# A state-space scan and a low-rank mixer on one Trainium2 core: the same steps in another listed order

## The chip, the cores and the metric

The kernel runs on one core of one Trainium2 chip. The metric is the device time of one execution in microseconds (us); the median of several executions counts, and lower is better.

The core has five engines, each with its own queue that it works off in order: PE (TensorE, matrix products; the profile shows the load of the stationary operand apart as PEld), DVE (VectorE), ACT (ScalarE), POOL (GpSimd) and SP (SyncE, which here only issues transfers, or DMAs, between the chip's large memory and the core's). Products land in PSUM, the accumulator memory, which the kernel uses as eight banks.

## What is computed

The reference chains two blocks over 4 batches of 768 tokens.

```python
# scan, per batch and head (8 heads, head_dim 32, d_state 16), in chunks of 32 tokens
cum = np.cumsum(np.log(np.clip(a, 1e-06, 1.0)), axis=-1)      # within the chunk
M = (Cc @ Bc.T) * np.exp(cum_i - cum_j) * (i >= j)
y = M @ xc + (Cc @ state) * np.exp(cum)
state = np.exp(cum[-1]) * state + sum_j(Bc_j * xc_j * np.exp(cum[-1] - cum_j))
# mixer, over x = the scan's output as (batch, 768, 256)
h = x.transpose(0, 2, 1) @ U @ V          # U: 768x32, V: 32x768
u = x + h.transpose(0, 2, 1)
out = u + np.maximum(u @ w_ch1, 0.0) @ w_ch2    # w_ch1: 256x1024, w_ch2: 1024x256
```

All inputs and the output are 32-bit floats.

## The kernel before

**Tiling.** The scan goes through 12 pairs, numbered k = 0 to 11: pair k belongs to batch k // 3 and covers 256 tokens (two blocks of 128). The mixer goes through half batches: batch b, half j (384 tokens). In it the hidden layer of 1024 has eight blocks m of 128.

**The order is written out by hand.** `tc.manual_schedule()` leaves the instructions of every engine in the order in which the program emits them, and the string `PLAN` gives that order as words. `follow(PLAN)` at the end splits it and calls one step a word: the letter picks the step, the numbers its arguments. A step emits instructions for several engines; what it emits is queued on each of them behind what the earlier words emitted there. A step that stands early in the list with its data late thus holds up all that stands behind it on the same engine. The words are:

- `Xk`, `Bk`, `wn` (and with a `Y` ahead `YXk`, `YBk`, `YU0`, `YV0`): loads, issued by SP (line 209). `X` is two transfers, `B` three (two of B, one of C), `w` one piece of a weight, `V` four. A load without `Y` also waits for the last VectorE instruction listed ahead of it (`hold`), which keeps it from running early. The framework gives SP's transfers eight semaphores in turn, so a ninth waits until the first of them has landed.
- `A0`, `A1`, `K0`: the decays from `a` (lines 384 to 411).
- `Pk`, or in parts `Qk.c`: B and C times decay (VectorE). `Tk` (twice), or `Vk.c.v`: PE transposes of that (line 496), copied out by ScalarE or VectorE.
- `sk`: PE products of B and x, the chunk's own state (line 570). `uk`: VectorE carries the state on, three or four instructions, and POOL masks it into `Sm` (line 597).
- `gk`: PE products of C and B (line 536). `mk`, `Mk`: VectorE masks them, two instructions each.
- `nk`, `jk`: PE products of M and x, first and second part (line 686). `ik`: PE products of C and the carried state (line 650). `yk`: ScalarE copies y out of PSUM. `tk`, `O0.0`, `O2.1`: PE turns it to tokens by columns (line 713), copied out by ScalarE, in `O2.1` by VectorE.
- The second part `jk` may run on PE only when the first part is known to have landed. If an instruction of another engine that depends on something after the first part has been emitted in between, that one is waited for. If not, `apart()` emits a copy of one column on POOL (`settled`, line 609) that waits for all products of `nk`, and `jk` waits for that copy.
- `cn` (three times): turns a weight's two 16-bit halves into a 32-bit float again: VectorE and ScalarE first, VectorE second, POOL third (line 439). `c0`, `C0` are the two halves of U and V, `c1` to `c5` pieces of `w_ch1` (`c1`, `c2` half a piece each), `c6` to `c9` pieces of `w_ch2`. `v0` spreads V (line 893). `Rn` (two or three times) splits a weight into three parts of type float32r for the up and down products of the later halves: ScalarE, POOL (line 453), VectorE.
- `pb`, `qb`: PE products with U and a second one that brings them to all rows (lines 739, 747, 757). `ab.j`: product with V; VectorE adds x to it, which gives u in `yT`.
- `U0.0.m`: the up product of block m for the first half of batch 0, in plain 32 bits (line 801). `Sb.j`: u in three parts. `fb.j.m`: up product of three parts, six PE instructions; `hb.j.m`: VectorE finishes what its relu leaves. `db.j.k.n`: the n-th piece of the down product for 128 tokens; the last piece is followed by a VectorE sum and the transfer of the output.
- `En`: n products of the 128 x 128 identity with n blocks of itself in one instruction (line 139), into a PSUM bank that is not read. They compute nothing that is used.

What one engine needs of another it waits for by semaphores that the framework places.

**Buffers.** Each PSUM tile takes its bank from the string `BANKS`, in the order of emission, and each staging tile of 4 KB a row (`words()`) takes one of 15 slots from `SLOTS`. A new tile waits until the last reader of the old one in its place is done. `u` in three parts has one buffer, which the plain copy of `w_ch1` holds until the products `U0.0.m` and the splits `R0` to `R3` are done.

The list before the change begins (the middle is left out):

```python
PLAN = (
    'E2 YX0 A1 YB0 A0 Q0.0 Q0.2 YB1 Q0.1 K0 YX1 Q1.0 YB2 V0.0.0 YB3 YX2 V0.1.1 s0 E1 u0 g0 E1 B4 '
...
    'd3.1.1.4 d3.1.2.2 d3.1.0.3 d3.1.2.3 d3.0.2.5 d3.1.1.5 d3.1.2.4 d3.1.2.5 d3.1.0.4 d3.1.0.5 ')
```

## Time and profile before

| | |
|---|---|
| median of 3 executions | 221.96 us (221.53 to 222.24) |
| the profiled execution, whole | 223.1 us |
| its span, first to last instruction | 221.4 us |
| mean clock granted to PE | 0.976 |
| PE busy | 210.0 us, 95% of the span |
| DVE, ACT, POOL busy | 151.7, 87.2, 35.8 us |
| transfers | 14.58 MB in 69663 packets, 63808 of them under 512 bytes |

How to read it: the times of all rows below come from the profiled execution, whose 223.1 us are 1.7 us more than its span and 1.1 us more than the median without the profiler. PE's busy time is a model, since products are pipelined: the start of one product to the start of the next is the better price of a step. The view by stages gives, for each stretch of time, the busy time and the number of instructions of each engine, the clock granted to PE (1.00 is full speed), the mean share of time in which the 16 DMA engines were busy, and GB/s. The view in order of time gives start, duration, engine, line, operation, output<-input, count, and in brackets how long the engine had been idle and whom it waited for.

### The profile page before, as it was taken

What the parts mean: (1) busy time and instruction counts of PE and PEld (TensorE: products, weight loads), DVE (VectorE), ACT (ScalarE), POOL (GpSimd) and SP (SyncE); (2) the same over time, 40 slices, a digit from 0 to 9 for tenths busy, and PEclk for the clock granted to TensorE, in tenths of its full rate; (3) what the DMA queues carried; (4) which work ended last, traced back from release to release, by engine and by line L of the source; (5) the groups of instructions that cost most, each with busy time, mean ns of one, the idle gap of its engine ahead of it and who ended that gap; (6) DMA issues with size and microseconds to landing.
All of it is one profiled execution on the core that took longest, in us unless ns stands there. A gap on an engine that the chain in (4) does not pass through costs nothing.

```text
span 221.4 us, 7025 instructions
## 1 busy us (share of the span) xinstructions
PE 210.0 (95%) x3054; PEld 186.6 (84%) x3054; DVE 151.7 (69%) x314; ACT 87.2 (39%) x196; POOL 35.8 (16%) x47
## 2 busy tenths in 40 slices
PE   7868989989999999999999999998999999999994
PEld 4645755666799799998999999997999999999993
DVE  4775787978987998669734788369315957745722
ACT  2343735768744754414733422133352223214000
POOL 3110036581443800100100010001000000000000
PEclk9995699999999999999999999999999999999999
DMA  6977853889854342216001110000000000010012
GB/s 98 130 100 126 177 175 98 118 135 202 160 153 60 47 95 40 35 52 115 12 0 31 43 50 27 3 24 28 0 3 25 27 24 0 3 47 24 0 50 95
DMA packets 69663, 14.58 MB, mean 66 GB/s; under 512 B 63808, under 2 KB 67840, under 8 KB 69632
## 3 DMA queue, kind: packets, MB, share of 16 engines
q1 hardware_dynamic: 69488, 14.06, 32.2%
q8 instruction: 24, 0.39, 0.7%
q10 hardware_dynamic: 144, 0.07, 0.1%
q14 instruction: 7, 0.06, 0.1%
HBM read 10.98 MB, written 3.15 MB: 64 GB/s over the span
## 4 chain that ended last, share of the span: by engine, by line
PE 74%; DVE 10%; DMA 4%; SPq 4%; issue 2%; POOL 2%; ACT 2%; POOLq 0%; DVEq 0%
PE x L801 34%; PE z L801 24%; DVE words L181 4%; SPq L209 4%; PE y L686 3%; PE y L650 3%; DMA bc<-in_C_dram 2%; PE w L496 2%; PE x L536 2%; DMA bc<-in_B_dram 2%; DVE S L181 1%; PE w L570 1%; DVE M L181 1%; PE w L713 1%; DVE yT L181 1%
## 5 line engine op out<-in xcount | busy, mean ns | idle before, releaser
L181 DVE SCALAR_TENSOR_TENSOR words<-words 128x768 fp32r<-128x768 f32 (+3 forms) x39 | 35.1, 903 | 4.0 <-PE z L801 1.3
L801 PE MATMUL z<-u,w 128*128 128x384 f32 x168 | 34.7, 343 | 0.0
L801 PE MATMUL x<-u,w 128*128 128x384 f32 x168 | 34.3, 342 | 0.0
L801 PE MATMUL x<-w,words 128*128 128x256 f32 x224 | 34.0, 285 | 0.0
L801 PEld LDWEIGHTS x<-w,words 128*128 128x128 f32 x224 | 30.5, 190 | 0.3
L801 PEld LDWEIGHTS z<-u,w 128*128 128x128 f32 x168 | 28.9, 188 | 0.5
L801 PEld LDWEIGHTS x<-u,w 128*128 128x128 f32 x168 | 28.7, 188 | 0.3
L825 ACT ACTIVATE words<-z 128x384 fp32r<-128x384 f32 x28 | 13.8, 492 | 36.0 <-PE z L801 36.0
L825 ACT ACTIVATE words<-x 128x384 fp32r<-128x384 f32 x28 | 13.7, 495 | 32.8 <-PE x L801 32.6
L181 DVE SCALAR_TENSOR_TENSOR words<-x,words 128x384 fp32r<-128x384 f32 x28 | 15.1, 552 | 16.2 <-ACT words L825 14.8
L801 PE MATMUL x<-w2c,words 128*128 128x256 f32 x144 | 25.5, 305 | 0.0
L801 PEld LDWEIGHTS x<-w2c,words 128*128 128x128 f32 x144 | 21.2, 189 | 0.7 <-issue 0.2
L597 POOL TENSOR_TENSOR Sm<-S,own 128x256 f32<-128x256 f32 (+1 forms) x12 | 7.8, 648 | 73.3 <-DVE S L181 73.1
L801 PE MATMUL z<-w,words 128*128 128x256 f32 x112 | 17.9, 287 | 0.5 <-DVE ytok L181 0.5
L181 DVE SCALAR_TENSOR_TENSOR words<-z,words 128x384 fp32r<-128x384 f32 x28 | 15.4, 550 | 3.6 <-ACT words L825 3.6
L801 PEld LDWEIGHTS z<-w,words 128*128 128x128 f32 x112 | 15.6, 189 | 1.2 <-DVE ytok L181 0.8
L181 DVE SCALAR_TENSOR_TENSOR ytok<-x,ytok 128x256 f32<-128x256 f32 (+1 forms) x17 | 6.7, 406 | 10.8 <-PE x L801 10.7
L181 DVE SCALAR_TENSOR_TENSOR S<-S,kept,w 128x64 f32<-128x64 f32 x40 | 11.2, 280 | 3.1 <-PE w L570 1.3
L181 DVE TENSOR_TENSOR BC<-bc,F 128x512 f32<-128x512 f32 (+2 forms) x18 | 10.0, 570 | 4.5 <-ACT F L391 2.1
L686 PE MATMUL y<-M,x 64*32 64x64 f32 x768 | 12.2, 232 | 0.7 <-POOL settled L609 0.6
L686 PEld LDWEIGHTS y<-M,x 64*32 64x32 f32 x768 | 8.9, 110 | 4.6 <-issue 1.8
L801 PE MATMUL z<-w2c,words 128*128 128x256 f32 x72 | 12.7, 306 | 0.0
(137 smaller groups left out, 332.7 us busy)
## 6 DMA issues: line engine op xcount, KB each, us to landing
words<-in_moe_w_ch_dram SPq DMA_DIRECT2D x7, 512.0 KB, 4.4
x<-in_x_dram SPq DMA_DIRECT2D x24, 128.0 KB, 3.2
out_dram<-ytok SPq DMA_DIRECT2D x23, 128.0 KB, 1.7
bc<-in_B_dram SPq DMA_DIRECT2D x24, 64.0 KB, 3.6
bc<-in_C_dram SPq DMA_DIRECT2D x12, 128.0 KB, 3.5
words<-in_moe_w_ch_dram SPq DMA_DIRECT2D x2, 256.0 KB, 4.2
words<-in_moe_U_dram SPq DMA_DIRECT2D x1, 192.0 KB, 3.2
words<-in_moe_V_dram SPq DMA_DIRECT2D x4, 48.0 KB, 2.7
```

The lines of the kernel that those rows point to most:

```text
L181: self.last = call(*args, **kwargs)
L209: op = issuer[0].dma_start(**kwargs)
L496: nc.tensor.transpose(out=tp[:, i, v], in_=s["BC"][:, i, c + v].rearrange("p h n -> p (h n)"), identity=ident)
L536: nc.tensor.matmul(out=s["g"][r][cols, c], lhsT=s["T"][rows, 0, c, cols], rhs=s["Cm"][rows, :, :, ts(2 * c + p, Q)].rearrange("r v t i -> ...
L570: nc.tensor.matmul(out=s["A"][p][ts(r, Q), v], lhsT=s["BC"][half, 0, v, 2 * r:2 * r + 2].rearrange("p h n -> p (h n)"), rhs=x_sb[k][half, ...
L597: nc.gpsimd.tensor_tensor(out=s["Sm"][:, sl], in0=s["S"][:, sl].rearrange("p i (s d) -> p i s d", s=2), in1=own2[:, b, 4 * q + sl.start:4 ...
L650: nc.tensor.matmul(out=channels(k)[r // 2][ts(r % 2, H), c, p], lhsT=own[ts(r, Q)], rhs=st[k]["T"][ts(r, Q), 1, :, ts(2 * c + p, Q)].rearr ...
L686: product = nc.tensor.matmul(out=y[n][ts(i, Q), c, p], lhsT=x_sb[k][half, c, h], rhs=s["M"][half, h // 2, c, h % 2], start=fresh(k, n, [i] ...
L713: nc.tensor.transpose(out=t[:, c, g], in_=yT[b][:, g, ts(2 * q + c, P)], identity=ident)
L801: nc.tensor.matmul(out=t, lhsT=lhsT, rhs=rhs, start=start, stop=True, skip_group_check=True)
L825: nc.scalar.activation(gs[j, m // 2][0][:, m % 2], t, AF.Relu, scale=NEAR)
```

## The change

`PLAN`, `BANKS` and `SLOTS` are replaced; nothing else is. The new list has all the words of the old one, each as often as before, in another order, and in addition three `E1` and one `E2`: products of the identity stand at eight places in place of four. Since PLAN rules all queues, all of PE, DVE, ACT, POOL and SP get a new order. Among what moves:

- The loads begin `X0 B0 B1 B2 B3 U X1 B5 w X2 V` in place of `X0 B0 B1 X1 B2 B3 X2 B4 U w V X3`.
- `g4`, `i3` and `a0.1`, listed ahead of the first `U0.0.m` before, stand behind it; `T5` and `g5` stand ahead of it.
- The eight `U0.0.m`, listed before ahead of `S0.1` and of any down product, now end only after six pieces of the plain down product of batch 0; `S0.1` and the `f0.1.m` follow after all but one of the twelve of these, where before they stood ahead of them.
- The helper `apart()` now emits `settled` eight times in place of three.

```diff
 PLAN = (
-    'E2 YX0 A1 YB0 A0 Q0.0 Q0.2 YB1 Q0.1 K0 YX1 Q1.0 YB2 V0.0.0 YB3 YX2 V0.1.1 s0 E1 u0 g0 E1 B4 '
-    'Q1.2 V1.0.2 m0 YU0 Q1.1 Q2.0 V1.1.2 s1 M0 n0 w0 Q2.2 YV0 u1 g1 m1 M1 i0 X3 Q2.1 w3 V2.0.2 j0 '
-    'y0 V2.1.3 n1 P3 g2 m2 P4 w1 s2 O0.0 M2 T3 T4 c0 u2 T3 i1 T4 j1 i2 c1 y1 g3 c1 n2 E1 j2 C0 y2 '
-    'C0 s3 m3 C0 t1 c0 c0 u3 w2 O2.1 v0 p0 M3 c4 c4 g4 c2 c2 q0 c2 n3 w4 c4 i3 m4 B5 a0.0 X4 c3 R2 '
-    'c3 a0.1 U0.0.1 c1 R2 R0 c3 R1 M4 X5 B6 U0.0.4 U0.0.0 U0.0.5 P5 c5 w6 U0.0.3 T5 T5 s4 j3 c5 R0 '
-    'y3 B8 c5 U0.0.2 u4 g5 R3 w5 i4 M5 X6 U0.0.6 B7 m5 n4 P6 n5 s5 R1 R3 w8 u5 c7 U0.0.7 j4 j5 S0.1 '
...
+    'E1 E1 YX0 A0 YB0 Q0.0 YB1 A1 Q0.2 Q0.1 K0 s0 YB2 YB3 Q1.0 V0.0.0 V0.1.1 Q1.2 YU0 YX1 Q1.1 u0 '
+    'Q2.0 E1 Q2.2 g0 m0 V1.0.2 B5 M0 V1.1.2 w0 V2.0.2 E2 n0 j0 g1 YX2 YV0 m1 i0 E1 P3 E1 M1 Q2.1 c0 '
+    's1 n1 u1 c0 T3 T3 E2 V2.1.3 c1 P5 j1 y0 i1 g2 m2 w1 O0.0 s2 c1 B4 y1 T5 u2 M2 T5 g3 C0 m3 i2 '
+    'n2 E1 X3 c0 j2 M3 y2 C0 c2 t1 C0 w3 c2 O2.1 v0 p0 s3 P4 T4 u3 X4 q0 c2 w2 T4 g5 a0.0 M5 X5 c4 '
+    'w5 m5 n3 c1 U0.0.1 U0.0.0 j3 g4 i3 c4 w6 c4 y3 m4 c3 s4 U0.0.4 R0 t3 U0.0.5 c3 c3 R1 u4 a0.1 '
+    'B6 U0.0.3 M4 c6 i4 w4 n5 c6 R0 n4 w7 c6 s5 U0.0.2 j4 j5 u5 y4 i5 c7 c7 y5 t4 d0.0.1.0 R4 t5 '
+    'd0.0.2.0 R1 p1 c5 d0.0.0.0 c5 w8 B7 c7 d0.0.2.1 P6 c8 T6 c8 R2 c5 X6 c8 R3 c9 T6 c9 q1 c9 '
+    'd0.0.1.1 d0.0.0.1 U0.0.6 U0.0.7 X8 R6 B10 P7 d0.0.1.2 d0.0.2.2 a1.0 R7 T7 T7 R3 d0.0.0.2 '
+    'd0.0.2.3 R2 d0.0.1.3 X9 g6 s6 S0.1 d0.0.0.3 f0.1.2 X10 M6 f0.1.4 f0.1.0 f0.1.1 u6 f0.1.5 R4 B9 '
...
```

## The prediction

> **What bounds the kernel now.** I read the page's busy times first, then stages cut where the work and the clock change, and last the chain and the single rows of the first 40 us.

> ```profile
> span 221.4 us, 7025 instructions
> PE 210.0 (95%) x3054; PEld 186.6 (84%) x3054; DVE 151.7 (69%) x314; ACT 87.2 (39%) x196; POOL 35.8 (16%) x47
> ```

> The stages (times from the start of the span; after each engine its busy time and number of instructions, then the clock, the DMA share and GB/s):

> ```profile
> 5.95:16.20 10.25, 7.67 (x231) 5.43 (x237) 7.59 (x27) 3.65 (x15) 1.50 (x3) 1.00 0.92 115
> 16.20:26.40 10.20, 8.89 (x222) 6.26 (x208) 7.21 (x23) 4.96 (x14) 0.62 (x2) 0.50 0.80 144
> 26.40:37.44 11.04, 9.88 (x293) 6.28 (x289) 8.04 (x24) 6.51 (x19) 4.62 (x7) 1.00 0.39 126
> 37.44:57.00 19.56, 19.00 (x368) 13.02 (x368) 17.70 (x34) 13.95 (x33) 10.05 (x10) 1.00 0.89 161
> 57.00:77.20 20.20, 19.72 (x168) 17.24 (x167) 17.96 (x32) 11.41 (x24) 11.71 (x9) 1.00 0.54 103
> 77.20:94.00 16.80, 16.77 (x173) 16.19 (x174) 13.47 (x25) 7.85 (x16) 1.39 (x2) 1.00 0.31 56
> 94.00:152.00 58.00, 58.00 (x1070) 54.93 (x1073) 39.57 (x83) 19.72 (x44) 2.89 (x5) 1.00 0.16 36
> 152.00:217.20 65.20, 64.61 (x572) 63.81 (x554) 37.01 (x62) 17.20 (x36) 0.97 (x1) 1.00 0.06 20
> ```

> From 37.44 us, where the first `U0.0.m` starts, PE idles 0.56 + 0.48 + 0.03 + 0 + 0.59 = 1.66 us in 179.8 us. There PE is the bound, and a new order of the same products can win little. Ahead of that PE has little to do and waits for data: two stages with 0.92 and 0.80 of the DMA engines busy, and one of 10.2 us at half the clock. So the change is priced by when the first `U0.0.m` starts, and by what is left for PE from there.

> ```profile
> 17.28 4.16 DMA bc<-in_B_dram
> 21.56 0.70 DVE BC L181
> ...
> 37.45 1.44 PE z L801 x4
> ```

> The chain shows a late transfer (`B4`), VectorE behind it, and PE's long run from 37.45 us.

> **The change, part by part.**

> *Loads.* Pair 1's x goes back six places in SP's queue, behind `B2`, `B3` and U; pair 2's x goes behind U, `X1`, `B5` and one w.

> ```profile
> 6.91 1.43 SPq L209 DMA_DIRECT2D x<-in_x_dram  x2
> ...
> 14.37 1.37 SPq L209 DMA_DIRECT2D x<-in_x_dram  x2
> ...
> 20.25 0.49 SPq L209 DMA_DIRECT2D words<-in_moe_w_ch_dram  x1
> 20.79 1.85 SPq L209 DMA_DIRECT2D words<-in_moe_V_dram  x4
> ...
> x<-in_x_dram SPq DMA_DIRECT2D x24, 128.0 KB, 3.2
> ...
> words<-in_moe_V_dram SPq DMA_DIRECT2D x4, 48.0 KB, 2.7
> ```

> Before, `X1` was issued from 6.91 and `X2` from 14.37. By its place in the queue (the DMA engines, not SP, set the pace, at shares of 0.92 and 0.80) `X1` now takes about the places of 13.74 to 14.96, and `X2` those just ahead of the four pieces of V, 20.2 to 20.8. With 3.2 us to landing `X1` is there at about 18 and `X2` at 20.8 + 3.2 = 24.0. `B5` also waits for the last of `m0`, and w and `X2` queue behind it; by its place it is issued about 15.5, later than `m0` can be done, so I cost that at nothing. If `m0` came after 15.5, every load behind it would slip by the difference.

> *From `X2` to the first `U0.0.m`.* What follows `X2` stands in this order on VectorE: `u2 M2 C0 m3 M3 C0`, then POOL's part of `C0`, which ends the conversion of V, then ScalarE's copy, then `v0` on PE.

> ```profile
> 19.83 0.65 PE L570 MATMUL w<-x,BC 64*32 64x64 f32 x24
> ...
> 22.17 0.75 DVE L181 TENSOR_TENSOR M<-z,causal 128x256 int32<-128x256 int32 x2
> ...
> 23.17 0.91 DVE L181 SCALAR_TENSOR_TENSOR S<-S,kept,w 128x64 f32<-128x64 f32 x3
> ...
> 25.19 0.42 DVE L181 TENSOR_SCALAR words<-words 128x192 f32<-128x192 f32 x2
> 25.64 0.36 DVE L181 SCALAR_TENSOR_TENSOR words<-words 128x192 int32<-128x192 int32 x1
> ...
> 28.22 1.26 POOL L439 TENSOR_TENSOR UV<-words 128x192 int32<-128x192 int32 x2
> ...
> 30.16 0.35 ACT L887 CAST Vn<-UV 128x192 fp32r<-128x192 f32 x1
> ...
> 30.56 0.35 PE L893 MATMUL y<-Vn,ident 32*32 32x192 f32 x2 [0.49 <-ACT Vn L887]
> ```

> 24.0 + 0.65 (`s2`) + 0.91 (`u2`) + 3 x 0.75 (`M2`, `m3`, `M3`) + 0.42 + 0.36 (`C0`) + 0.63 (half of the 1.26) + 0.35 (ScalarE) = 29.6, against the 30.56 of before: 1.0 us earlier. From there to the first `U0.0.m` it was 37.44 - 30.56 = 6.88 us. Of that `q0` loses 0.2 us less: `g4` no longer stands ahead of it, and its operand was ready at 33.94.

> ```profile
> 33.55 0.39 ACT L752 ACTIVATE pT<-w 128x256 f32<-128x256 f32 x1
> ...
> 34.16 0.70 PE L757 MATMUL w<-pT,spot 128*128 128x256 f32 x2
> 34.79 0.45 PE L686 MATMUL y<-M,x 64*32 64x64 f32 x32
> 35.17 0.64 PE L650 MATMUL y<-T,Sm 32*64 32x64 f32 x24
> 35.78 0.44 PE L767 MATMUL x<-Vs,ps 128*128 128x384 f32 x1
> ...
> 43.89 0.60 PE L496 MATMUL w<-ident,BC 128*128 128x128 f32 x4
> 44.42 0.45 PE L570 MATMUL w<-x,BC 64*32 64x64 f32 x32
> ```

> So the first `U0.0.m` starts at 36.2: 1.2 us earlier. The bounds: if `X2` is as early as before, V sets the pace, whose last piece is issued by 20.79 + 1.85 = 22.64 and landed by 25.3. With 0.42 + 0.75 + 0.75 + 0.36 + 0.63 + 0.35 behind it `v0` starts at 28.6, 2.0 us earlier, and with the 0.2 of `q0` 2.2 us are won in place of 1.2. The other end is `X2` two places later in the queue, 0.6 us each (1.37 for the two of `X2`): nothing won.

> *What is left for PE from there.* Moved behind it: `g4`, `i3` (35.78 - 35.17 = 0.6) and `a0.1` (0.35, by the two products of `a0.0`, 0.7 at most); moved ahead: `T5` (44.42 - 43.89 = 0.5) and `g5`. The two g cancel. That is 0.6 + 0.35 - 0.5 = 0.45 us more. It lies in PE's bound stage, so all of it counts.

> *Four more instructions of identity products.*

> ```profile
> 3.67 1.06 PE L139 MATMUL w<-ident 128*128 128x256 f32 x2
> ...
> 27.75 0.49 PE L139 MATMUL w<-ident 128*128 128x128 f32 x2
> ```

> Three `E1` at 0.45 to 0.49 and an `E2` at about 1.0: 2.5 us at most. All stand ahead of `X2`'s products or of `j2`, where PE waits: two lie just ahead of `s1`, which now waits for `X1` until 18, and the `E2` ahead of `j1`. I take 0; 2.5 us is the other end, if those waits were gone.

> *Five more `settled` copies on POOL.*

> ```profile
> POOL settled L609 <- PE y L686: 20.6, 3, 12.2
> ...
> PE y L686 <- POOL settled L609: 0.6, 1, 0.6
> ```

> Three cost PE 0.6 us in one place before. Now there are eight, each behind what POOL has listed ahead of it, and on PE all behind `jk` waits. Ends: 0 and 5 x 0.6 = 3.0 us. Those of `j0` to `j2` fall where PE waits for x, `j3` has two `U0.0.m` between its parts, so I take 0, with `j4` as a rival.

> *Half the clock.* Before, full speed in 5.95 to 16.20 with PE 7.67 of 10.25 us busy was followed by 10.2 us at half, and those with 8.89 of 10.20 by full speed to the end. In the new list the identity products fill waits in both stretches, and `s1` and `s2` leave new ones. I take the same state up to 26.4 as before: on the path above only `s2` is PE's, and its 0.65 is a row at half clock.

> ```profile
> PE x L496 <- DVE S L181: 1.1, 1, 1.1
> ```

> [...]

> Sum: -1.2 + 0.45 + 0 + 0 = about -0.75, with the range of the parts mostly on the slow side. The execution of 223.1 us becomes 222.35, and the median without the profiler, 1.1 us below it, 221.96 - 0.75 = 221.2.

> **The rivals.**

> 1. *Slower: half the clock lasts on past 26.4, over `i2` to `a0.0`.* For it: PE now waits for `X1` to 18 and again for `X2` from about 22 to 24, inside the stretch that before was 8.89 of 10.20 busy and earned full speed. Against: the added identity products. On the path are `v0` (32.44 - 30.56 = 1.9), `p0` (1.0), `q0` (0.35 for its two), `a0.0` and half of `j2`, `t1`, `O2.1`: some 3 us that would double: 221.2 + 3 = 224.2. It decides from about 0.75 us of added time, a quarter of that stretch.
> 2. *A new wait: `j4` behind POOL.* Its `settled` is listed behind POOL's part of `c6`, which needs two VectorE steps of `c6`, themselves behind `u4`, `a0.1` and `M4`.

> ```profile
> L439 POOL TENSOR_TENSOR w2c<-words 128x512 int32<-128x512 int32 x4 | 5.8, 1474 | 9.1 <-DVE words L181 7.6 <-ACT words L825 1.5
> ```

> One such step is 1.47 us, and before POOL waited 7.6 us for VectorE at this line. If PE gets to `j4` as POOL begins it, 1.47 us are lost: 222.7. Against: VectorE is less loaded there.

> 3. *Faster: fewer waits from 37 to 77 us.* There VectorE was busy 17.70 + 17.96 of 39.76 us, 90%, and PE idled 0.56 + 0.48. `S0.1` and the `h` steps now come some ten down pieces later, which takes load off VectorE there. If that idle time of 1.04 us goes and V's end of the bounds above holds (1.0 us more), it is 221.2 - 1.0 - 1.0 = 219.2. Against: PE already was 97% busy there.

> **How the numbers follow.** Chances: the forecast, 220.4 to 222.0, 0.42; rival 1 0.23; rival 2 0.13; rival 3 0.22. About 0.3%, 0.66 us, is what a measurement here can tell from no change. The forecast gives faster 0.22 and same 0.2; rival 1 slower; rival 2 slower 0.09, same 0.04; rival 3 faster. Together faster 0.44, same 0.24, slower 0.32. The range runs from rival 3's 219.2, less 0.4 for the spread of the runs shown (221.53 to 221.96), to rival 1's 224.2.

> **What would show it.** Right: `s1` starts at about 18 and `s2` at about 24, waiting for a DMA; `v0` at 29.6 and the first line-801 product at 36.2; PE over 98% busy after it; full clock from 26.4. Wrong: a later half-clock stretch (rival 1); a wait of line 686 for `settled` near 48 us (rival 2); a first `U0.0.m` at 35 or less, or the last product less than 180 us behind it (rival 3).

## The result, and the profile after

The changed kernel takes 219.77 us (median of 7 executions, 218.88 to 220.50), the kernel before 222.20 us in the same call: a ratio of 0.989, with a 95% interval of 0.9854 to 0.9926. (Here and below, a ratio leaves out executions more than 1.5% above the fastest of their kernel, while a median counts them.) The forecast was 221.2 us. The profiled execution took 220.5 us with a span of 218.8, against 223.1 and 221.4 before: 2.6 us less, where the sum of the prediction had 0.75. Line numbers are one higher than before (line 802 is the old 801).

The page's first rows, and the same stages as in the prediction (busy time and count of PE, PEld, DVE, ACT and POOL, then clock, DMA share, GB/s):

```profile
span 218.8 us, 7028 instructions
PE 210.3 (96%) x3062; PEld 187.0 (85%) x3062; DVE 151.0 (69%) x314; ACT 87.7 (40%) x196; POOL 35.6 (16%) x52
```

```profile
5.95:16.20 10.25, 9.15 (x180) 6.47 (x188) 6.15 (x20) 4.95 (x17) 1.38 (x3) 1.00 0.96 128
16.20:26.40 10.20, 9.50 (x291) 6.79 (x276) 7.90 (x26) 4.91 (x14) 1.21 (x3) 1.00 0.61 118
26.40:37.44 11.04, 10.17 (x262) 6.22 (x257) 8.79 (x26) 5.51 (x17) 3.70 (x8) 1.00 0.70 133
37.44:57.00 19.56, 19.02 (x404) 13.38 (x403) 16.08 (x35) 12.70 (x27) 11.07 (x10) 1.00 0.65 175
57.00:77.20 20.20, 20.20 (x193) 17.37 (x191) 17.08 (x29) 12.29 (x26) 10.21 (x9) 1.00 0.81 131
77.20:94.00 16.80, 16.80 (x196) 16.45 (x191) 15.26 (x27) 8.00 (x18) 2.15 (x2) 1.00 0.19 28
94.00:152.00 58.00, 57.55 (x1089) 54.84 (x1088) 39.47 (x82) 21.16 (x49) 3.82 (x7) 1.00 0.14 32
152.00:215.00 63.00, 63.00 (x476) 62.50 (x476) 37.41 (x62) 16.50 (x33) 0.00 (x0) 1.00 0.06 20
```

The stage of 16.20 to 26.40, at half the clock before, is at full speed. PE's idle time between 37.44 and the last product is 0.54 + 0 + 0 + 0.45 + 0 = 0.99 us, against 1.66.

Single rows in order of time, of the changed kernel (PE):

```profile
18.06 0.46 PE L571 MATMUL w<-x,BC 64*32 64x64 f32 x32
...
23.95 0.43 PE L571 MATMUL w<-x,BC 64*32 64x64 f32 x24
...
30.38 0.35 PE L894 MATMUL y<-Vn,ident 32*32 32x192 f32 x2 [0.51 <-ACT Vn L888]
...
36.02 1.21 PE L802 MATMUL z<-yT,w1f 128*128 128x384 f32 x3
...
215.21 0.28 PE L802 MATMUL x<-ps,Vs 128*128 128x256 f32 x1
```

and the last product of the kernel before:

```profile
217.81 0.28 PE L801 MATMUL x<-ps,Vs 128*128 128x256 f32 x1
```

The first `U0.0.m` comes at 36.02 in place of 37.44 (1.42 us earlier). From there to the last product it is 215.21 - 36.02 = 179.19 in place of 217.81 - 37.44 = 180.37 (1.18 less). These are the 2.6 us. The new waits for `settled` are there too (who waited for whom: total, times, longest):

```profile
PE y L687 <- POOL settled L610: 1.3, 3, 0.5
```

So there are three questions: why the clock stayed up, what took 1.18 us out of a stretch that was forecast to grow by 0.45, and what the waits for `settled` cost.

### The profile page after: what moved, and what is told of

Its sections match the earlier page's. It is cut to its first block, busy times and chain, and to the rows that moved or that the text cites. A ratio compares the mean times of both kernels' runs of the same rounds, so it can differ in the third digit from the quotient of the medians.

```text
span 218.8 us, 7028 instructions
## 1 busy us (share of the span) xinstructions
PE 210.3 (96%) x3062; PEld 187.0 (85%) x3062; DVE 151.0 (69%) x314; ACT 87.7 (40%) x196; POOL 35.6 (16%) x52
## 4 chain that ended last, share of the span: by engine, by line
PE 88%; DVE 8%; issue 1%; POOL 1%; DVEq 0%; POOLq 0%
PE x L802 38%; PE z L802 27%; PE y L687 4%; PE y L651 2%; PE x L537 2%; PE w L497 2%; DVE words L182 2%; PE w L714 2%; DVE S L182 2%; DVE M L182 2%; PE w L571 1%; PE w L140 1%; PE x L140 1%; PE w L740 1%; PE z L537 1%
## 5 line engine op out<-in xcount | busy, mean ns | idle before, releaser
L182 DVE SCALAR_TENSOR_TENSOR words<-words 128x768 fp32r<-128x768 f32 (+3 forms) x39 | 35.9, 919 | 5.1 <-PE z L802 3.4
L802 PE MATMUL x<-u,w 128*128 128x384 f32 x168 | 33.8, 340 | 0.0
L802 PE MATMUL z<-u,w 128*128 128x384 f32 x168 | 33.0, 340 | 0.0
L826 ACT ACTIVATE words<-z 128x384 fp32r<-128x384 f32 x28 | 13.7, 491 | 25.3 <-PE z L802 25.3
L802 PE MATMUL z<-w,words 128*128 128x256 f32 x112 | 18.4, 287 | 0.0
L802 PE MATMUL z<-w2c,words 128*128 128x256 f32 x72 | 13.2, 307 | 0.0
L687 PEld LDWEIGHTS y<-M,x 64*32 64x32 f32 x768 | 8.3, 105 | 5.5 <-POOL settled L610 2.8
L687 PE MATMUL y<-M,x 64*32 64x64 f32 x768 | 11.6, 223 | 1.4 <-POOL settled L610 1.3
L182 DVE TENSOR_TENSOR M<-x,causal 128x256 int32<-128x256 int32 x24 | 9.0, 416 | 4.7 <-PE z L537 3.3
## 6 DMA issues: line engine op xcount, KB each, us to landing
x<-in_x_dram SPq DMA_DIRECT2D x24, 128.0 KB, 3.1
out_dram<-ytok SPq DMA_DIRECT2D x23, 128.0 KB, 1.7
bc<-in_C_dram SPq DMA_DIRECT2D x12, 128.0 KB, 3.0
```

The source lines that it names most:

```text
L182: self.last = call(*args, **kwargs)
L687: product = nc.tensor.matmul(out=y[n][ts(i, Q), c, p], lhsT=x_sb[k][half, c, h], rhs=s["M"][half, h // 2, c, h % 2], start=fresh(k, n, [i] ...
L802: nc.tensor.matmul(out=t, lhsT=lhsT, rhs=rhs, start=start, stop=True, skip_group_check=True)
L826: nc.scalar.activation(gs[j, m // 2][0][:, m % 2], t, AF.Relu, scale=NEAR)
```

## Experiments

### The identity products and the clock

One list without the four places that the change added (shown), one without any identity products, and the changed kernel once more:

```diff
-... V2.0.2 E2 n0 j0 g1 YX2 YV0 m1 i0 E1 P3 E1 M1 ... T3 T3 E2 V2.1.3
+... V2.0.2 n0 j0 g1 YX2 YV0 m1 i0 P3 M1 ... T3 T3 V2.1.3
```

> The changed list without the identity products that the change added (E2 ahead of n0, the E1 on both sides of P3/M1 ahead of s1, E2 ahead of V2.1.3); the order of all other words, banks and slots are those of the changed kernel. No result of these products is read. Theory A (the added products keep the granted clock full in the head): the clock falls to half for about 10 us somewhere between 16 and 28 us as in the kernel before, the first line-802 product comes 1 to 2 us later than 36.02, and the time is 221 to 222 us against 219.8. Theory B (the order alone is the gain, the four places only fill waits): the clock stays full, the first line-802 product lies within 0.3 us of 36.0, and the time is 219.3 to 220.0.

> The changed list with no identity product at all (all eight places out, order, banks and slots else unchanged). Theory A (these products hold the clock): the clock is at half for 10 us or more of the head, the first line-802 product comes 2 to 4 us later than 36.02, and the time is 222 to 224 us. Theory B (they fill waits and do nothing to the clock): the time is 219.3 to 220.0.

> The changed kernel once more, beside the next three on one chip. Theory A (clock): 0.987 to 0.991 of the kernel before, and a granted clock of 0.997 to 1.000 in nearly every run, where the list with four places only had 0.977 to 0.991 in all of its 12 runs; the two then differ by some 1 us because of the clock. Theory B (the difference of 0.989 to 0.9925 was that of two chips): this run stands at 0.992 to 0.994, with clocks below 0.99 among its runs.

Measured: with four places 221.32 us, ratio 0.9925 (0.9894 to 0.9956); with none 221.24, ratio 0.9965 (0.9929 to 1.0001); the changed kernel again 220.35, ratio 0.9903 (0.9868 to 0.9938), as theory A of its expectation has it. The intervals of the first and the third overlap, but the clocks do not: 0.999 or 1.000 in all 15 executions of the changed kernel, 0.977 to 0.991 in all 12 with four places. Before, 29 executions of one call had 0.969 to 0.999. The first line-802 product with four places:

```profile
36.81 1.53 PE L802 MATMUL z<-yT,w1f 128*128 128x384 f32 x4
```

That is 0.8 us later than in the two traces of the changed kernel (36.02 and 35.97), while the way from there to the last product is the same within 0.15 us. Theory A has the mechanism right and its price too high: the clock is at half for 3.4 us in place of about 10, and the product comes 0.8 us later in place of 1 to 2. With none, full speed had begun 2 us earlier, at about 9.05; the clock is at half for 6.8 us, the product came at 36.37, and the time of 221.24 lies between the two theories, so neither of their prices holds.

The mean clock of an execution does not give its time. At 0.999 or 1.000 the kernel before took 220.90 to 222.61 us (seven executions of three calls, median 221.57) and the changed kernel 218.88 to 220.51 (median 220.26); with four places the five executions at 0.991 took 219.37 to 221.40. So the fall of the clock is a part of the gain, 0.8 us by these traces; without it the changed kernel is still some 1.3 us faster.

When the clock falls is seen if the time is cut where it changes. The stages of the list with four places (PE's busy time stands behind the length, the clock third from the end):

```profile
14.37:17.78 3.41, 2.95 (x152) 2.21 (x150) 1.36 (x4) 0.89 (x3) 0.18 (x1) 1.00 0.83 120
17.78:21.19 3.41, 1.71 (x30) 1.01 (x30) 3.23 (x13) 1.33 (x3) 0.78 (x2) 1.00 0.86 156
21.19:24.60 3.41, 3.35 (x100) 2.74 (x100) 1.79 (x6) 1.34 (x4) 0.01 (x1) 0.50 0.51 102
24.60:28.00 3.40, 3.40 (x106) 2.50 (x112) 2.58 (x9) 2.63 (x7) 1.07 (x2) 1.00 0.66 132
```

of the changed kernel:

```profile
18.02:21.44 3.42, 2.80 (x80) 1.77 (x87) 2.52 (x11) 1.32 (x3) 0.79 (x2) 1.00 0.80 159
```

and of the kernel before:

```profile
12.79:16.20 3.41, 2.04 (x103) 1.49 (x92) 2.04 (x8) 0.60 (x4) 0.51 (x1) 1.00 0.64 83
16.20:19.61 3.41, 2.53 (x98) 1.63 (x80) 2.15 (x7) 1.52 (x6) 0.11 (x1) 0.50 0.83 118
19.61:23.02 3.41, 2.98 (x48) 2.21 (x34) 2.22 (x7) 0.84 (x2) 0.00 (x0) 0.50 0.80 185
23.02:26.43 3.41, 3.41 (x98) 2.46 (x100) 2.84 (x11) 2.63 (x7) 0.51 (x1) 0.50 0.76 131
```

Each later stretch at half the clock lasts a multiple of 3.41 us (3.4, 6.8 or 10.2), in all seven traces that have one. It begins behind a piece of 3.41 us in which PE was busy 1.71 or 2.04 us, and ends behind one with 3.35 or 3.41, not behind 2.53 or 2.98. Over all traces with a fall:

```
trace                    PE busy in the 3.41 us before the fall   PE busy in the last 3.41 us at half
before                   2.04                                     3.41
four places              1.71                                     3.35
no identity products     2.34                                     3.40
two more in the old list 1.79                                     3.40
x loads moved, old list  1.62                                     3.40
changed, then before     0.94                                     3.35
before, then changed     1.71                                     3.42
```

At full speed, no piece with 2.39 us or more of PE work was followed by a fall in these traces. Below that these busy times, which are modelled, give no exact bound: a piece with 2.34 was followed by a fall, but pieces with 2.20 (none, from 9.05 us), 1.95 (two more in the old list, from 52.51) and 1.93 (second trace of four more in the old list, from 48.80) were not. With the added products the piece at this place has 2.80 us in place of 1.71, and no fall follows it. Two of these falls came without a long wait of PE: in the kernel before, the longest between 5.9 and 26.5 us was 1.1 us (the row `PE x L496 <- DVE S L181` of the prediction), and with four places no wait of PE between 8 and 24 us was longer than 0.7 us.

### The same products in the old order

```diff
-... V0.1.1 s0 E1 u0 g0 E1 B4 ... i0 X3 Q2.1 w3 V2.0.2 j0 y0
+... V0.1.1 s0 E1 E1 u0 g0 E1 B4 ... i0 E2 X3 Q2.1 w3 V2.0.2 j0 E1 y0
```

(and an `E1` ahead of the first `T4`; a second list has only the `E1` behind `s0` and the one behind `j0`).

> The list of before with four more places of identity products put at its own waits (E1 behind s0, E2 behind i0, E1 behind j0, E1 ahead of the first T4); nothing else moves. Theory A (the added products keep the clock full): the half clock of 16.2 to 26.4 us goes, and with it 1 to 1.5 us: 220.7 to 221.2 against 222.2. Theory B (the order alone is the gain): the clock stays full or not with no change of the time above 0.3 us, 221.9 to 222.5.

> The list of before with two more places of identity products (E1 behind s0, E1 behind j0). TensorE's own instructions come in blocks of 256: in the traces so far every idle time of TensorE that waited for nothing visible ended at instruction 193 + a multiple of 256 (961, 1473 and 1985 in the list with four more places, 1729 in the one before), 1.3 to 1.6 us behind the end of a 16 KB transfer on the instruction queue. Theory F (the four more places filled the head, but by the same token TensorE ran into the blocks' loading): with two more places idle times again lie at 193 + 256 k only, together between 0.5 and 3.4 us ahead of 58 us, the first line-802 product comes 0 to 0.8 us earlier than before's 37.44, and the time is 222 to 225 us. Theory A (identity products in waits keep the clock and cost nothing behind): 221 to 222 us.

> A second trace of the list of before with four more places, whose first trace was its fastest run. Theory F (block loading): idle times again end at instruction 961, 1473 and 1985, and their sum is larger where the time is longer. Theory G (something else varies): the idle times of the first trace (0.59, 1.05, 1.70 us) stay as they were and the time that is added lies elsewhere.

Measured: four more 224.75 us, ratio 1.0089 (1.0055 to 1.0123); two more 224.82, ratio 1.0096 (1.0061 to 1.0130); the second trace of four more 224.03 us. Neither theory of the first expectation holds: the time got longer. With four more places the clock was full (1.000) in both traces, as in four of the list's 12 executions, and the first line-802 product came 0.8 us earlier, at 36.62 and 36.66, as theory A has it. But behind it 0.97 us were lost, 217.96 - 36.62 = 181.34 in place of 180.37. PE stands still without waiting for anything that the profile shows ("issue"). Rows of PE, four more places:

```profile
25.79 0.29 PE L537 MATMUL z<-Cm,T 32*64 32x128 f32 x1 [0.29 <-issue]
...
35.15 0.35 PE L651 MATMUL y<-T,Sm 32*64 32x64 f32 x4 [0.83 <-issue]
...
51.51 0.30 PE L571 MATMUL w<-x,BC 64*32 64x64 f32 x4 [1.48 <-issue]
```

two more places:

```profile
24.06 1.09 PE L497 MATMUL w<-ident,BC 128*128 128x128 f32 x4 [3.71 <-DVE BC L182]
...
54.54 1.56 PE L802 MATMUL z<-yT,w1f 128*128 128x384 f32 x4 [1.46 <-issue]
```

and the kernel before, where the same line of the waits was 0.6 us:

```profile
48.11 0.78 PE L650 MATMUL y<-T,Sm 32*64 32x64 f32 x31 [0.56 <-issue]
```

PE's recorded instructions (products, weight loads and its queue's own waits for semaphores) can be counted, and set beside the transfers of 16 KB on the instruction queue, of which each of these traces has 24. The fourth column goes from the start of the instruction before to the start of this one, so it holds more than the idle time in the brackets above (all times in us):

```
list                     PE instruction   starts at   behind last one    transfer ended   later than that by
before                   1729             48.11       0.79               46.53            1.58
four more                 961             25.79       0.59               24.47            1.32
four more                1473             35.14       1.05               33.72            1.42
four more                1985             51.50       1.70               50.13            1.37
four more, second trace  1473             35.19       0.78               33.70            1.49
four more, second trace  1985             52.15       1.70               50.75            1.40
two more                 1473             37.47       0.67               36.02            1.45
two more                 1729             49.52       0.91               48.10            1.42
two more                 1985             54.54       1.67               53.23            1.31
x loads moved, old list  1729             48.96       0.78               47.63            1.33
```

All of these numbers are 193 plus a multiple of 256. By this count one transfer brings the block of 256 instructions that PE needs next, and PE goes on 1.3 to 1.6 us after it has landed, in stops of 0.6 to 1.7 us. Theory F holds in where the stops lie; for the first product of the list with two more, and for the sum in the second trace, it does not. In the changed kernel no wait is put down to "issue"; such an instruction starts at most 0.32 us behind the last one (the 1985th, at 48.04, 1.85 us behind its transfer).

With two more places the 3.71 us that PE waited for VectorE, which waited for a transfer of B, made the first product 1.2 us late (38.66); this is another loss, that of the loads below. The second trace of four more has the same 1.70 us, and 0.64 in a new place, the 1729th, where the first has 0.03; that is 0.61 of the 0.77 us by which its way from the first line-802 product to the last is longer (218.77 - 36.66 = 182.11). Ahead of that product it stood less (0.20 and 0.78 us for 0.59 and 1.05), so the sum over the whole is the same, 3.3 us. So the stops take back what the clock had given, and in the first trace no more than that: its last product comes at 217.96, against 217.81 before. That the median of four more, 224.75, is above both traces (223.23 and 224.03) goes with the clock: the four executions at 0.999 or 1.000 took 223.23 to 224.26 us, the other eight, at 0.977 to 0.992, took 223.78 to 227.01. Where it fell in those eight, with these products in the list, was not seen.

### The order of the loads

Two words moved alone, into the old list, and back in the new one:

```diff
-... K0 YX1 Q1.0 YB2 V0.0.0 YB3 YX2 V0.1.1 ... m0 YU0 Q1.1
+... K0 Q1.0 YB2 V0.0.0 YB3 YX1 V0.1.1 ... m0 YU0 YX2 Q1.1
...
-... K0 s0 YB2 YB3 Q1.0 ... YU0 YX1 Q1.1 ... g1 YX2 YV0
+... K0 YX1 s0 YB2 YB3 YX2 Q1.0 ... YU0 Q1.1 ... g1 YV0
```

> The list of before with only two words moved: pair 1's x behind B3 and pair 2's x behind U, as in the changed list. In every trace with the head of before, VectorE waited for a transfer of B or C (0.9 to 3.5 us), in none with the changed head. Theory L (the x loads ahead of B and C cost the head): VectorE's waits for bc fall below 0.3 us, the first line-802 product comes 0.5 to 1.2 us earlier than 37.44, the time is 221.2 to 222.0 against 222.4, ratio 0.994 to 0.998. Theory M (the loads matter only together with the steps that use them): s1 and s2, which stand as early as before, now make TensorE wait for x, the first product is not earlier, ratio 0.999 to 1.010.

> The changed list with only these two words moved back: pair 1's x behind K0, pair 2's x behind B3, as before the change. Theory L: VectorE waits for bc again, 1 us or more in all, the first line-802 product comes at 36.8 to 38 in place of 36.0, the time is 220.5 to 222, ratio 0.993 to 0.999. Theory M (VectorE's steps, not the loads, set the head): no wait for bc above 0.3 us reaches TensorE, the first product stays within 0.4 us of 36.0, ratio 0.988 to 0.992.

Measured: moved in the old list 226.21 us, ratio 1.0118 (1.0078 to 1.0159); moved back in the new list 222.75, ratio 0.9984 (0.9945 to 1.0023). In the old list VectorE no longer waits for B or C, but PE does for x:

```profile
PE w L571 <- DMA x<-in_x_dram: 3.4, 2, 2.9
```

and the first product came at 38.25. Theory M's mechanism is there, with a ratio just above its range. In the new list neither theory holds, though the ratio lies in theory L's range. Its trace shows no wait of VectorE for B or C, so theory L's mechanism is wrong; ScalarE waits for U instead:

```profile
ACT words L435 <- DMA words<-in_moe_U_dram: 4.2, 1, 4.2
```

That traced execution lost only 0.45 us up to the first product (36.46). But of its 12 executions the five with a clock of 0.999 or 1.000 took 220.70 to 221.13 us, and the seven with 0.969 to 0.992 took 222.70 to 223.73. So the new place of two loads is worth some 2 us in the median, and most of that goes with the clock. Where in those seven the clock fell was not seen. The new steps without the new loads gain next to nothing, and the new loads without the new steps cost 1%.

### The waits for `settled`

```diff
-... w7 c6 s5 U0.0.2 j4 j5 ...  M9 j8 f1.1.0 ...  s10 j9 u10 d1.1.1.2 u11
+... w7 s5 U0.0.2 j4 c6 j5 ...  M9 f1.1.0 j8 ...  s10 d1.1.1.2 j9 u10 u11
```

> The changed list with three words moved: c6's last part behind j4 (so that POOL takes settled for j4 ahead of that conversion), j8 behind f1.1.0, and d1.1.1.2 ahead of j9. It aims at the three waits of line 687 for settled that the changed kernel shows (0.61 us ahead of j4, 0.38 ahead of j8, 0.65 ahead of j9). Theory A (PE is the bound and every one of these waits is on the path that sets the end): the waits go and the time falls by 1.0 to 1.6 us, to 218.2 to 218.8. Theory B (a wait of PE that is filled comes up again at the next thing PE is early for): the three waits go but others grow by as much, and the time stays within 0.4 us of 219.8.

> The list with c6's last part behind j4, j8 behind f1.1.0 and d1.1.1.2 ahead of j9 once more, now beside the changed kernel on one chip. Theory A (the waits for settled lie on the path): 0.5 to 1.3 us below the changed kernel of the same call. Theory B (they come up again elsewhere): within 0.3 us of it. The first trace showed 0.66 us less from the first line-802 product to the last product, because the three moves also put other words side by side.

Measured: 219.07 us, ratio 0.985 (0.9809 to 0.9891), and 219.79, ratio 0.9893 (0.9855 to 0.9932), the changed kernel beside the latter 220.35. Of the 1.3 us of waits of line 687 in the changed kernel, 0.34 lies in the head (15.44 us), 0.54 ahead of `j4` and 0.39 ahead of `j9`. Here only the one in the head is left:

```profile
PE y L687 <- POOL settled L610: 0.3, 1, 0.3
```

From the first line-802 product to the last it is 213.02 - 34.50 = 178.52 and 214.51 - 36.02 = 178.49, against 179.19: 0.7 us less of the 0.9 that went there. The first expectation's theory A (218.2 to 218.8) asked for too much; the second's, 0.5 to 1.3 us below the changed kernel of the same call, is met with 0.6, though the intervals overlap. This list has the lowest medians of the study.

What one of these waits was made of (changed kernel, in order of time, PE, DVE and POOL):

```profile
134.63 0.95 DVE L182 TENSOR_TENSOR u<-yT,u 128x768 fp32r<-128x768 f32 x1
134.87 0.76 POOL L610 COPY settled<-slot 128x1 f32<-128x1 f32 x1 [12.87 <-PE y L687]
...
135.68 0.46 PE L687 MATMUL y<-M,x 64*32 64x64 f32 x32 [0.39 <-POOL settled L610]
```

The copy of one column, 0.18 us in the median of eight, took 0.76 and ended within 0.05 us of VectorE's instruction. What held it is not shown: no run here took VectorE's instruction away. But all 14 traces show the pattern: the copies that took over 0.3 us ended 0.03 to 0.06 us behind a VectorE instruction; all others took 0.17 to 0.19, those beside VectorE's masks (`M<-x,causal`, `M<-z,causal`) among them.

The first trace also shows what an early start of full speed is worth. The two products of `K0` on line 400 took 0.59 us there, and the first line-802 product came at 34.50; in the second trace, with the same list, and in the changed kernel, whose head is the same, they took 1.01, at half speed, and the product came at 36.02:

```profile
6.57 0.59 PE L400 MATMUL z<-la,middle 128*128 128x192 f32 x2
```

against, in the changed kernel,

```profile
6.68 1.01 PE L400 MATMUL z<-la,middle 128*128 128x192 f32 x2
```

### The two lists spliced

The changed list up to `S1.1` (104 us) with the rest in the order of before, and the list of before up to `S1.0` (77 us) with the rest in the changed order. At the seam 49 and 62 of some 250 tiles also had to take another PSUM bank, and 40 and 44 of 120 another slot.

```diff
 ... d1.0.1.1 d1.0.2.1 d1.0.1.2
-S1.1 d1.0.2.2 f1.1.4 M8 P9 d1.0.2.3 d1.0.1.3 ...
+P9 u8 i8 M8 n8 X11 j8 s9 S1.1 y8 T9 T9 ...
```

> The changed list up to S1.1 (103.9 us in the changed kernel's profile), the words that are left in the order of before; banks and slots else as in the changed kernel. Theory A (the gain behind the first line-802 product was made ahead of 104 us: by the prices of step pairs the excess behind that point is 1.9 us in the changed kernel and 1.9 in the one before): the time is the changed kernel's within 0.3 us, ratio 0.988 to 0.991. Theory B (the order of the later half carries it): the ratio is 0.993 to 0.996.

> The list of before up to S1.0 (77 us in its profile), the words that are left in the order of the changed kernel. Theory A (the gain is made ahead of 77 us and between 77 and 104): the head stays that of before with its half clock, the first line-802 product at 37 to 38 us, and what is left of the gain is at most 0.5 us: ratio 0.997 to 1.001. Theory B (the order of the later half carries the gain): 0.993 to 0.996.

Measured: 233.06 us, ratio 1.0485 (1.0441 to 1.0529), and 232.10, ratio 1.0463 (1.0416 to 1.0511). In both runs both theories fell. PE's waits of the first:

```profile
PE w L571 <- DMA x<-in_x_dram: 2.4, 2, 1.4
PE y L687 <- POOL settled L610: 2.3, 4, 0.8
PE x L802 <- DVE ytok L182: 1.7, 1, 1.7
```

The 2.4 us for x lie in the head of this execution, ahead of 36 us and of the seam. Of the stretch from the first line-802 product to the last, 191.40 us in place of 179.19, PE idles 0.55 up to 104 us, 5.5 from 104 to 152 and 3.8 from 152 on, in many waits. The splice does not say in which half the gain was made, nor whether the loss comes from the order or from the tiles that had to change place; and no run here changes `BANKS` and `SLOTS` alone.

## Why the prediction was right, and where it was not

*The sign and the range* were right, the size was not: -0.75 forecast, -2.6 in the trace. The outcome lies between the forecast and rival 3 (219.2), whose mark, a last product less than 180 us behind the first `U0.0.m`, is there (179.19); its other mark, a first `U0.0.m` at 35 or less, is not.

*The first `U0.0.m`*: 36.02 against 36.2 is luck: errors of 0.8 and 1.0 us cancel. `v0` came at 30.38, not 29.6. In place of the sum's steps:

```profile
24.99 0.91 DVE L182 SCALAR_TENSOR_TENSOR S<-S,kept,w 128x64 f32<-128x64 f32 x3 [0.49 <-PE w L497]
...
28.58 0.34 DVE L182 SCALAR_TENSOR_TENSOR words<-words 128x192 int32<-128x192 int32 x1
...
29.05 0.73 POOL L440 TENSOR_TENSOR UV<-words 128x192 int32<-128x192 int32 x1 [1.08 <-ACT yT L705]
...
29.49 0.58 ACT L722 COPY ytok<-w 128x512 f32<-128x512 f32 x1
29.96 0.37 ACT L888 CAST Vn<-UV 128x192 fp32r<-128x192 f32 x1
```

`u2` waited for PE and began at 24.99 where the sum had 24.65 (0.34); VectorE's steps from there took what was priced. POOL began at 29.05 where the sum had 28.62 (0.43, with the 0.34), took 0.73 for 0.63 (0.10), and ScalarE, busy with another copy, began 0.18 after POOL's end: 0.7 of the 0.78. The sum had left out PE's wait and ScalarE's queue. From `v0` on it was 5.64 us where the sum had 6.88 - 0.2 = 6.68, 1.24 less than before in place of 0.2. `q0`, the one step that the sum changed, came only 0.08 sooner behind `p0`. `v0` itself went from 1.88 to 1.20 up to `p0`: in the kernel before PE stopped in it at its 1217th instruction, at 31.93, which starts 0.38 us behind the last one and 1.24 behind the end of its transfer. And `a0.0` to the first `U0.0.m` went from 1.66 to 1.18: VectorE's two instructions of `m4`, which stood between `a0.0` and its sum before, are gone from there.

```profile
35.76 0.76 DVE L181 TENSOR_TENSOR M<-x,causal 128x256 int32<-128x256 int32 x2
```

That is a row of the kernel before; the prediction had not followed it, nor the stop in `v0`.

*`s1` at about 18 and `s2` at about 24* came out to the tenth (18.06, 23.95), by luck again: neither waited for a DMA, PE was late with what is listed ahead. The step that failed is the place in the queue. The prediction gave `X2` the issue times that its place had before, 20.2 to 20.8, and 24.0 for its landing; SP was there 2.6 us earlier, and the transfer had landed at 22.62 (`X1` at 16.54):

```profile
17.56 1.10 SPq L210 DMA_DIRECT2D x<-in_x_dram  x2
```

*"What is left for PE from there", +0.45* is the term that failed: -1.18. Let each step be priced by the median time from its start to that of the next one, over all steps of its kind in both traces. Up to the start of the last step, the new order's own price is then 0.5 us higher (173.6 against 173.1), as forecast; the rest is time beyond these prices, 6.8 us before and 5.2 after. (The split hangs on the pricing. Priced by pairs of neighbouring steps, where a pair that occurs once counts as its own price, both orders have 2.8 us beyond it, and the own price is the one that falls. The 1.18 us do not hang on it.) Of the 1.65 us that went by the first pricing, 0.67 is idle time in the profile, 0.99 us in place of 1.66. Before, PE stood 0.56 us ahead of `i4`, for the block with the 1729th instruction, 0.50 ahead of a down piece, waiting for VectorE,

```profile
77.23 0.98 PE L801 MATMUL z<-w,words 128*128 128x256 f32 x6 [0.50 <-DVE ytok L181]
```

and 0.59 for `settled` ahead of `j11`; after, it stood 0.54 and 0.39 for `settled`. Another 0.9 lies at up and down steps (`f`, `d`) without an idle time in the profile: before, seven of them took 0.17 to 0.19 us more than their kind, after, two. What these waited for is not seen, and no run here tests which part of the new order removed it; so the cause of the 1.18 us stays open in this part. The sentence "a new order of the same products can win little" took PE's busy share for the bound; but busy time is modelled, and it hid steps that were longer than their kind.

*The identity products at 0 (end 2.5 us dearer)*: by the traces they earn: the list without the four places reached the first line-802 product 0.8 us later. An end below nothing was missing.

*"The same state up to 26.4 as before"* was wrong in both directions: half speed lasted to about 11 us at the start (the transposes of line 497 start 0.213 us apart at 9.8 and 0.109 apart at 12.3) in place of 5.96, and did not come back. Rival 1 feared a longer half clock from PE's new waits; the products that fill them decided it the other way.

*The five more copies at 0*: PE's waits for them went from 0.6 to 1.3 us, 0.9 of it behind the first `U0.0.m`. Rival 2 is there in kind: `settled` stood behind POOL's 1.61 us of `c6`, and PE idled ahead of `j4`,

```profile
47.40 1.61 POOL L440 TENSOR_TENSOR w2c<-words 128x512 int32<-128x512 int32 x1 [2.00 <-PE w L571]
...
48.96 0.38 POOL L610 COPY settled<-slot 128x1 f32<-128x1 f32 x1
...
49.39 0.86 PE L687 MATMUL y<-M,x 64*32 64x64 f32 x64 [0.54 <-POOL settled L610]
```

for 0.54 us in place of the 1.47 priced. The wait ahead of `j9` had not been seen.

## What to carry to other kernels

Price an order by what each stretch costs beyond its own products, start to start, and not by the busy share of a modelled engine: a stretch that was 99% busy gave up 1.2 us here. In a head that waits for data, ask of every window of 3.41 us whether PE is busy for 2.4 us of it, above which the clock never fell in these traces: cheap products in the right place kept the clock and were worth 0.8 us in the trace. The same kind of products in the other order made the kernel 1% slower: in the traces PE stood 3.3 us for its own instructions, and in eight of 12 executions the clock fell all the same. And take a searched order as one thing: two loads moved back cost most of its 1%, and a splice of two good orders cost 5%.
